# Two memory-attention layers and two linear-attention layers on one core: other queues, places and release points for stores and loads

## The chip, the core and the metric

The kernel runs on one core of a Trainium2 chip. The core has a matrix engine (TensorE, PE in the profile, with its weight loads shown as PEld), a vector engine (VectorE, DVE), a scalar engine (ScalarE, ACT), a general engine (GpSimd, POOL) and a synchronisation engine (SyncE, SP), which here only issues DMAs. DMAs are also issued by ScalarE and GpSimd. The metric is the device time of one execution in microseconds (us); lower is better.

## The reference

The input `x` has 2048 rows of 640 values. Four layers follow one another, A B A B, each on a layer norm of its input and with its input added to its output.

```python
# layer A: recurrent memory attention, 32 heads of 192, 64 segments of 32 rows, 8 memory rows
mem = mem0
for s in range(n_seg):
    h = concatenate([mem, x[segment s]])              # 8 + 32 rows
    q, k, v = h @ Wq, h @ Wk, h @ Wv                  # per head
    p = softmax(where(mask, q k^T * scale, -1e9))
    o = (p v, all heads) @ Wo
    mem = o[:8]                                       # goes into the next segment
    outs.append(o[8:])
# layer B: linear attention with softmax features, over all rows at once
```

So the segments of an A layer form a chain: segment s+1 needs the first eight output rows of segment s. Layer B has no such chain.

## The kernel before

An A layer has two stages. `A_pre` is the batched stage. In it the kernel computes, for eight rows of every segment (the border rows, whose input does not depend on the memory), the keys, queries and values of all segments in large matmuls, and puts them into DRAM: keys and queries into `kqb_d`, values into `vb_d`. `A_chain` is the chain. It goes through the 64 segments one after another, each in four rounds of eight heads; every other segment takes the rounds in reverse order.

The batched stage. `keys_and_queries(h, r)` makes the keys and queries of half h of the segments for round r: 120 matmuls (L985), evictions by VectorE and ScalarE in turn (L94 and L96, through `evict`), and one store of 1.5 MB to `kqb_d` (L993). Eight of them run in each A layer, mixed with four `first_values`, which make the border values of the first segments. In the first layer the stage also does the layer norm of all 2048 rows in 16 blocks: `norm_tasks` cuts a block into four steps (load of the rows at L926, moments, deviation, applying at L302 and store to `xn` at L927), and `evict` does one such step after each eviction. The normed block stands in a tile `ln_xn`. GpSimd issues the block's load and store. In the third layer the rows were normed before.

Also in the first layer, `lay_out_wo` (L812 to L816) rewrites the output weights `Wo` in DRAM, 32 DMAs from SP, into the order in which the chain reads them (`wo_rows`); `early_wo` and `late_wo` load parts of that (L774) into SBUF (the large tile is called `arena`). `fetch_first_rows` (L1000) is SP's DMA that brings the first segment's normed rows into `under`. At the start of the chain VectorE transposes them into `hT` (L1081), copies the kept tokens into `tT` (L1082), and prepares the banks of the first queries and keys (L1090).

A segment of the chain. Per round, `project` (L1137 to L1159) multiplies `hT` with the weights of queries, keys and values: five steps (b = 0 to 4, one for each 128 rows of the weights) of four matmuls each (L1154). Then come ScalarE's copies of the raw rows (L1169, L1181), transposes (L1174), scores (L1191), the weighted values (L1204), the turning of the result (`turn`, with L1382 for round 1, which writes it into the buffer `vt`), and the product with `Wo` (L1263), which collects in `ps_w`. The segment ends with the sum of that product (L1457), which gives the next `hT` (L1459). GpSimd fetches the border keys and queries of a round (`load_kqb`, L1123), copies them beside the others (L1130), and fetches the border values into `Vp` (L1134).

Streamed weights. Of four rounds' weights most stay in SBUF. Three of Q's five row blocks, two of K's and two of V's of the first and last round share seven slots (`SLOTS`, `load_slot`, L748), and four pieces of `Wo` share a region as well (`load_piece`, L797). So each segment loads 11 pieces again, for its last round. They are put in the list `held`, in the order Q, Q, Q, K, K, V, V and four of `Wo`, and `release` takes the next from the list: SP's DMA then waits for a given matmul. `PACE` says at which step: `("Q", 1): 4` means that after step 4 of the projection of Q in round 1 one load is released.

Border values of later segments. They are computed during the chain by `next_values` (into the bank `ps_x`). `keep_values` (L1301) copies them by ScalarE (L1304) into `vt` and gives back a function that stores `vt` into `vb_d` (L261, SP's queue). At the start of a segment the copy stands first, ahead of the summed rows (`keep_rows`, L1112), the tails (`tail_rows`, L1247) and the first query rows; the store is issued behind the projection of Q. This happens in 112 segments of the two chains.

The order of instructions on each engine is that in which the program issues them; an engine waits at an instruction until what it needs is there, and everything behind it on that engine waits too.

Of the kernel before, what the change touches and what calls it, by code (L numbers as in the profile page):

```python
# [8 lines left out]
P = 128  # L9
BF16 = mybir.dt.bfloat16  # L10
# [12 lines left out]

VH = 194

PACE = {("Q", 0): 0, ("K", 0): 1, ("V", 0): 3, ("Q", 1): 4, ("K", 1): 4, ("V", 1): 3, ("Q", 2): 1, ("K", 2): 0, ("V", 2): 0,
        ("Q", 3): 0, ("K", 3): 0}

STEPS = (2, 5)

# [92 lines left out]
class Kernel:  # L123
# [712 lines left out]
    def A_pre(self, xn_dram, li, load_matrix, piece, wo_mid, wo_end, lay_out_wo, early_wo, x_raw):  # L836


        nc, tc, ev, KC, NSEG = self.nc, self.tc, self.ev, self.KC, self.NSEG
        NR = 4  # L840
        SH = min(NSEG, 32)
# [8 lines left out]
        with ExitStack() as es:  # L850
            ps_ = es.enter_context(tc.tile_pool(name=f"A{li}_preps", reuse_waits="tile", bufs=8, space=bass.MemoryType.PSUM))
            if x_raw is not None:
                lp = es.enter_context(tc.tile_pool(name=f"A{li}_preln", reuse_waits="tile", bufs=2))
# [27 lines left out]
            def norm_tasks(load, done, tag="ln_xn"):  # L881

                v = {}

                def a():
                    v["x"] = lp.tile([P, self.Dm], BF16, name="ln_x", bufs=3)
                    load(v["x"])

                def b():
                    v["m"] = self.ln_moments(lp, v["x"])  # L890

                def c():
                    v["d"] = self.ln_deviation(lp, v["m"])

                def d():
                    xn = lp.tile([P, self.Dm], BF16, name=tag, tag=tag)
                    self.ln_apply(lp, v["x"], v["m"], v["d"], xn[:])
                    done(xn)

                return [a, b, c, d]  # L900
# [72 lines left out]
            def keys_and_queries(h, r):  # L973
                nonlocal turn
                st = sts[turn % 2]
                turn += 1
                xBT = columns(h)
                for mi, m in enumerate("KQ"):
                    w = [piece(m, r, b) for b in range(KC)]
                    for c0 in range(0, 12, CB):  # L980
                        ps = ps_.tile([P, 512], F32, name="ps_pre", tag="bank")
                        for i in range(CB):
                            c = c0 + i
                            for b in range(KC):
                                nc.tensor.matmul(ps[:, T * i:T * i + T], lhsT=w[b][:, P * c:P * c + P], rhs=xBT[:, b, :],  # L985
                                                 start=(b == 0), stop=(b == KC - 1))
                        G, xi = c0 // 6, c0 % 6
                        so = st[:, :, 96 * mi:96 * mi + 96]
                        so = (so.rearrange("p s (i g t) -> p i g s t", g=2, t=8) if m == "K" else
                              so.rearrange("p s (i t g) -> p i g s t", g=2, t=8))  # L990
                        evict(out=so[:, xi:xi + CB, G],
                              in_=ps[:, :].rearrange("p (i t s) -> p i s t", i=CB, t=8))
                nc.scalar.dma_start(out=self.kqb_d[r, :, SH * h:SH * h + SH, :], in_=st)  # L993

            def load_round(r):
                for m in "KQV":
                    load_matrix(m, r)

            def fetch_first_rows():
                nc.sync.dma_start(out=self.first_rows(), in_=self.rows_of(0))  # L1000

            if x_raw is not None:
                load_round(3)
                load_round(2)
                rows_ready(0)
                tasks += tails(1)
                keys_and_queries(0, 3)
                rows_ready(1)
                tasks += all_rows()
                keys_and_queries(1, 3)  # L1010
                first_values(3)
                self.build_A_consts()
                load_round(1)
                load_round(0)
                for r in (0, 2, 1):
                    lay_out_wo([r])
                early_wo(True)
                lay_out_wo([3])
                fetch_first_rows()
                keys_and_queries(0, 2)  # L1020
                keys_and_queries(1, 2)
                first_values(2)
                keys_and_queries(0, 1)
                keys_and_queries(1, 1)
                first_values(1)
                keys_and_queries(0, 0)
                first_values(0)
                keys_and_queries(1, 0)
                early_wo(False)
            else:  # L1030
                load_round(0)
                rows_ready(0)
                load_round(2)
                keys_and_queries(0, 0)
                first_values(0)
                self.build_A_consts()
                keys_and_queries(0, 2)
                rows_ready(1)
                keys_and_queries(1, 0)
                load_round(3)  # L1040
                load_round(1)
                early_wo(True)
                fetch_first_rows()
                keys_and_queries(1, 2)
                first_values(2)
                keys_and_queries(0, 3)
                keys_and_queries(1, 3)
                first_values(3)
                load_round(0)
                keys_and_queries(0, 1)  # L1050
                first_values(1)
                keys_and_queries(1, 1)
                early_wo(False)
# [4 lines left out]
    def A_chain(self, xn_dram, at_dram, li, load_slot, piece, late_wo, load_both, wo, low):  # L1058
        nc, tc, KC, NSEG = self.nc, self.tc, self.KC, self.NSEG
        scale = float(self.Dh) ** -0.5  # L1060
        NR = 4
        with tc.tile_pool(name=f"A{li}_ch", reuse_waits="tile", bufs=1) as sp, \
# [74 lines left out]
            def project(hT, ps, m, n, s, steps):  # L1137
                order = rounds(s)
                r = order[n]
                ns = SLOTS[m]  # L1140
                for i in steps:
                    b = (i + KC - ns) % KC if n == 0 else i
                    w = piece(m, r, b)
                    for g in range(4):
                        if m == "V":
                            hp = 2 * (g % 2) + g // 2
                            rhs = w[:, 384 * hp:384 * hp + 384]
                        else:
                            w3 = w[:, 32 * g:32 * g + 32]
                            rhs = ap3(w3, [list(w3.ap[0]), [P, 6], [768, 2], [1, 32]])  # L1150
                        o = ps[32 * g:32 * g + 32, 0:384]
                        if m != "V":
                            o = ps[32 * g:32 * g + 32, :].rearrange("p (x c) -> p x c", x=2)[:, :, 64 * (g // 2):64 * (g // 2) + 192]
                        last = nc.tensor.matmul(o, lhsT=hT[:, b, :], rhs=rhs, start=(i == 0),  # L1154
                                         stop=(i == KC - 1), tile_position=(0, 32 * g), skip_group_check=True)
                    if n == 0 and b >= KC - ns:
                        self.held.append(lambda b=b: load_slot(m, order[NR - 1], b))
                    if PACE.get((m, n)) == i:
                        self.release(last)  # L1159
# [12 lines left out]
            def turn_rows(pairs):  # L1172
                for o, i in pairs:
                    nc.vector.transpose(out=o, in_=i)  # L1174
# [126 lines left out]
            def keep_values():  # L1301
                if waiting:
                    ps, k, unit = waiting.pop()
                    nc.scalar.activation(out=self.two_heads(vt), in_=ps[:, 0:384].rearrange("p (e f) -> p e f", e=2), func=ACT.Copy)  # L1304
                    return lambda: self.store_values(nc.sync, vt, k, *unit)
# [24 lines left out]
            for s in range(NSEG):  # L1330
# [4 lines left out]
                def q_or_k(m, n, halves=False):  # L1335
                    ps = psk if m == "K" else psq
                    project(hT, ps, m, n, s, range(KC))
                    return to_rows(ps, m, halves)
# [7 lines left out]
                    elif s + 1 < NSEG:  # L1346
                        extra_v(s + 1, n + 2 - NR)

                store = None
                if s > 0:  # L1350
                    store = keep_values()
                    keep_rows(W_done)
                    rows = tail_rows(rct, spare_rows())
                    otb = turn_tail(rows)
                    store_rows(s - 1)
                    store_tail(otb, s - 1, rounds(s - 1)[L])
                raw = q_or_k("Q", 0)
                if store:
                    store()
                turn_rows(raw)  # L1360
                turn_rows(q_or_k("K", 0))
                if s == 0:
                    late_wo(3, range(OWN // 2))
                pv = v_banks()
                project(hT, pv, "V", 0, s, range(KC))
                v_rows(pv, 0, "sv")
                turn_tails(s)
                OTs = []
# [186 lines left out]
```

## Time and profile before

| | us |
|---|---|
| median of 3 runs | 3292.88 (3291.52 to 3293.26) |
| the profiled execution | 3279.86 |
| span in its trace | 3278.1 |
| TensorE busy | 3043.7 |
| VectorE busy | 2157.5 |
| ScalarE busy | 1901.7 |
| GpSimd busy | 1384.0 |

The span is the time from the first to the last instruction in the trace; the execution's own time is 1.76 us more. The mean granted clock of TensorE is 0.986 of full speed. A line such as L1154 is a line of the kernel printed above. Rows of waits give an engine and line, what it waited for, the total in us, how often, and the longest. Rows of a timeline give the start in us, the duration, the engine, the line, the operation, the tiles (out<-in), the count, and in brackets the idle time before it and what ended it. A row of a window gives its bounds, its length, the busy time of TensorE, its weight loads, VectorE, ScalarE and GpSimd, each with a count, TensorE's clock, the busy share of the DMA engines and GB/s.

### The profile page before, as it was taken

The numbers are of one execution on the slowest core, as the hardware profiler recorded it, in microseconds if no ns is written. First come the engines' busy times: TensorE is split into PE (matmuls) and PEld (weight loads), VectorE is DVE, ScalarE is ACT, GpSimd is POOL, SyncE is SP. The second block draws the span as 40 slices with busy tenths as digits, with TensorE's granted clock in tenths as the row PEclk, the third lists the DMA queues.
The fourth block names the chain that finished last, engine by engine and source line by source line (L and its number), as shares of the span: only waits on it lengthen the run. The fifth ranks groups of instructions, "written<-read, shape, count | busy, mean of one in ns | idle before, by whom it ended". The sixth has DMA issues, their size and how long they took to land.

```text
span 3278.1 us, 141616 instructions
## 1 busy us (share of the span) xinstructions
PE 3043.7 (93%) x59586; PEld 1930.3 (59%) x59586; DVE 2157.5 (66%) x5425; ACT 1901.7 (58%) x4537; POOL 1384.0 (42%) x2856
## 2 busy tenths in 40 slices
PE   8799999999999999999999999999999999998999
PEld 6555566566566555555467566665566565655553
DVE  5466677677677667746654666667677667776565
ACT  2256666666666666646443566666666666665463
POOL 2254455445554454530121554545454545454300
PEclk9899999999999999999999999999999999999999
DMA  9877777777777777760268777777777777777400
GB/s 376 294 267 237 234 254 253 235 243 259 243 243 257 243 236 247 258 224 3 97 222 325 259 243 238 242 253 245 231 245 257 245 239 245 259 237 265 158 1 33
DMA packets 338750, 749.67 MB, mean 229 GB/s; under 512 B 68538, under 2 KB 115250, under 8 KB 335042
## 3 DMA queue, kind: packets, MB, share of 16 engines
q1 hardware_dynamic: 268258, 637.09, 56.2%
q0 software_dynamic: 66976, 77.87, 8.6%
q10 hardware_dynamic: 2880, 25.66, 1.9%
q8 instruction: 469, 7.68, 0.9%
q14 instruction: 167, 1.37, 0.1%
HBM read 670.77 MB, written 78.01 MB: 228 GB/s over the span
## 4 chain that ended last, share of the span: by engine, by line
PE 60%; DMA 25%; DVE 7%; issue 3%; ACT 3%; POOL 0%; SPq 0%; POOLq 0%; DVEq 0%; ACTq 0%
DMA arena<-in_A_Wv_dram 17%; PE ps_qk_q L1154 9%; PE ps_w L1263 9%; PE ps_v L1154 9%; PE ps_qk_k L1154 8%; PE ps_pre L985 5%; PE ps_s L1191 4%; PE kv L1510 2%; DMA vb<-under 2%; PE ps_o L1204 2%; DVE raws L1457 2%; PE ps_wo L466 2%; DMA Vp<-vb 2%; DMA arena<-in_A_Wk_dram 1%; PE ps_pq L517 1%
## 5 line engine op out<-in xcount | busy, mean ns | idle before, releaser
L1154 PEld LDWEIGHTS <-hT 128*32 128x32 bf16 x30720 | 801.6, 97 | 540.8 <-issue 98.0
L1174 DVE STREAM_TRANSPOSE QK<-raws 128x512 bf16<-128x512 bf16 (+1 forms) x1152 | 712.5, 634 | 133.1 <-ACT raws L1169 102.2
L1154 PE MATMUL ps_qk_q<-arena,hT 128*32 128x384 bf16 x10240 | 512.0, 328 | 54.1 <-DVE hT L1459 25.5
L1130 POOL COPY QK<-kqb 64x192 bf16<-64x192 bf16 x1024 | 351.9, 344 | 456.7 <-DMA kqb<-kqb 205.6
L1154 PE MATMUL ps_qk_k<-arena,hT 128*32 128x384 bf16 x10240 | 515.7, 328 | 6.4 <-DMA arena<-in_A_Wk_dram 3.8
L1154 PE MATMUL ps_v<-arena,hT 128*32 128x384 bf16 x8192 | 447.0, 328 | 43.0 <-DMA arena<-in_A_Wv_dram 35.1
L1169 ACT ACTIVATE raws<-ps_qk_k 128x512 bf16<-128x512 f32 (+1 forms) x640 | 313.6, 511 | 246.3 <-PE ps_qk_k L1154 240.1
L1234 ACT ACTIVATE raws<-ps_o,under 128x192 bf16<-128x192 f32 x1024 | 374.4, 421 | 119.4 <-DVE under L1228 98.9
L1134 POOL DMA_DIRECT2D Vp<-vb x512 | 258.9, 506 | 384.1 <-PE ps_t L1217 174.7
L1169 ACT ACTIVATE raws<-ps_qk_q 128x512 bf16<-128x512 f32 x512 | 305.0, 596 | 127.6 <-PE ps_qk_q L1154 116.1
L1183 DVE CAST Vp<-ps_v 64x384 bf16<-64x384 f32 x512 | 286.3, 559 | 71.4 <-ACT Vp L1181 57.8
L1263 PE MATMUL ps_w<-arena,under 128*32 128x320 bf16 x6144 | 310.0, 301 | 14.4 <-issue 11.8
L1123 POOL DMA_DIRECT2D kqb<-kqb x512 | 288.6, 564 | 68.4 <-POOL QK L1130 59.4
L1181 ACT ACTIVATE Vp<-ps_v 64x384 bf16<-64x384 f32 x512 | 247.1, 483 | 91.3 <-PE ps_v L1154 89.3
L1191 PEld LDWEIGHTS <-QK 128*80 128x80 bf16 x4096 | 196.8, 121 | 162.8 <-issue 152.4
L1191 PE MATMUL ps_s<-QK 128*80 128x80 bf16 x4096 | 255.0, 210 | 6.5 <-POOL QK L1130 2.9
L1273 ACT ACTIVATE E<-ps_s 80x320 bf16<-80x320 f32 x512 | 218.0, 426 | 37.3 <-PE ps_t L1217 36.9
L1119 POOL DMA_DIRECT2D attn<-under x128 | 91.5, 715 | 339.6 <-DVE under L1115 317.5
L985 PEld LDWEIGHTS <-arena 128*128 128x128 bf16 x1920 | 189.3, 99 | 43.1 <-issue 15.3
L1304 ACT ACTIVATE under<-ps_x 128x384 bf16<-128x384 f32 x112 | 55.1, 492 | 273.3 <-PE ps_x L257 273.3
L1204 PE MATMUL ps_o<-Vp,E 80*32 80x193 bf16 x4096 | 181.6, 249 | 23.3 <-DMA Vp<-vb 10.9
L1263 PEld LDWEIGHTS <-under 128*32 128x32 bf16 x6144 | 149.5, 96 | 45.2 <-issue 19.9
(167 smaller groups left out, 4378.8 us busy)
## 6 DMA issues: line engine op xcount, KB each, us to landing
arena<-wo_rows SPq DMA_DIRECT2D x560, 320.0 KB, 6.2
arena<-in_A_Wq_dram SPq DMA_DIRECT2D x427, 384.0 KB, 6.2
arena<-in_A_Wk_dram SPq DMA_DIRECT2D x298, 384.0 KB, 6.5
arena<-in_A_Wv_dram SPq DMA_DIRECT2D x290, 384.0 KB, 7.0
kqb<-arena ACTq DMA_DIRECT2D x16, 1536.0 KB, 9.4
kqb<-kqb POOLq DMA_DIRECT2D x512, 48.0 KB, 5.0
Vp<-vb POOLq DMA_DIRECT2D x512, 24.2 KB, 4.7
otb<-otb POOLq DMA_DIRECT2D x256, 48.0 KB, 4.4
```

Source lines behind the costliest of these rows:

```text
L985: nc.tensor.matmul(ps[:, T * i:T * i + T], lhsT=w[b][:, P * c:P * c + P], rhs=xBT[:, b, :], start=(b == 0), stop=(b == KC - 1))
L1123: nc.gpsimd.dma_start(out=kqb[:], in_=self.kqb_d[r, :, s, :])
L1130: nc.gpsimd.tensor_copy(out=o, in_=kqb[h, :].rearrange("p (x c q) -> p x c q", c=3, q=16))
L1134: nc.gpsimd.dma_start(out=Vs[n % 2][64:80, :], in_=self.vb_d[s // 8, r].rearrange("g (t s) x f -> s (g t) (x f)", s=8)[s % 8])
L1154: last = nc.tensor.matmul(o, lhsT=hT[:, b, :], rhs=rhs, start=(i == 0), stop=(i == KC - 1), tile_position=(0, 32 * g), skip_group_check=True)
L1169: nc.scalar.activation(out=raw[:, c], in_=ps[:, c], func=ACT.Copy)
L1174: nc.vector.transpose(out=o, in_=i)
L1183: nc.vector.tensor_copy(out=o, in_=i)
L1191: nc.tensor.matmul(S[0:80, c0:c0 + 80], lhsT=KT[:, 4 * x + c, :], rhs=QT[:, 4 * x + c, :], start=(c % 2 == 0), stop=(c % 2 == 1), skip_gro ...
L1204: nc.tensor.matmul(O[G][32 * h:32 * h + 32, VH * G:VH * G + 193], lhsT=E[0:80, 80 * h + 32 * G:80 * h + 32 * G + 32], rhs=V[0:80, VH * h:V ...
L1234: nc.scalar.activation(out=out, in_=i, func=ACT.Copy, scale=rc[G])
L1263: step = nc.tensor.matmul(W[q:q + 32, 0:320], lhsT=OT[i // 6][:, i % 6 // 2, 32 * (i % 2):32 * (i % 2) + 32], rhs=rhs, start=(first and i ...
```

## The change

It does five things.

1. `PACE`: the releases at Q of round 1, and K and V of round 1 come at steps 3, 1 and 1 in place of 4, 4 and 3; those at K and V of round 2 and Q and K of round 3 at step 3 in place of 0.
2. The tile `ln_xn` of the first layer's layer norm has three buffers in place of two.
3. The 16 stores of keys and queries to `kqb_d` (L993) are issued by GpSimd in place of ScalarE.
4. `fetch_first_rows` is called earlier: in the first layer ahead of the 32 DMAs of `lay_out_wo`, in the third ahead of `early_wo(True)`. The order of the laying out stays (rounds 0, 2, 1, then 3).
5. `keep_values` is called after the keys of the first round in place of the segment's start, so that ScalarE copies the border values behind the first keys' rows; the store follows the projection of V on SP, behind the third load of Q.

```diff
-PACE = {("Q", 0): 0, ("K", 0): 1, ("V", 0): 3, ("Q", 1): 4, ("K", 1): 4, ("V", 1): 3, ("Q", 2): 1, ("K", 2): 0, ("V", 2): 0,
-        ("Q", 3): 0, ("K", 3): 0}
+PACE = {("Q", 0): 0, ("K", 0): 1, ("V", 0): 3, ("Q", 1): 3, ("K", 1): 1, ("V", 1): 1, ("Q", 2): 1, ("K", 2): 3, ("V", 2): 3,
+        ("Q", 3): 3, ("K", 3): 3}
...
-                    xn = lp.tile([P, self.Dm], BF16, name=tag, tag=tag)
+                    xn = lp.tile([P, self.Dm], BF16, name=tag, tag=tag, bufs=3 if tag == "ln_xn" else 2)
...
-                nc.scalar.dma_start(out=self.kqb_d[r, :, SH * h:SH * h + SH, :], in_=st)
+                nc.gpsimd.dma_start(out=self.kqb_d[r, :, SH * h:SH * h + SH, :], in_=st)
...
                 load_round(0)
-                for r in (0, 2, 1):
-                    lay_out_wo([r])
+                fetch_first_rows()
+                lay_out_wo((0, 2, 1))
                 early_wo(True)
                 lay_out_wo([3])
-                fetch_first_rows()
...
                 load_round(1)
+                fetch_first_rows()
                 early_wo(True)
-                fetch_first_rows()
...
-                store = None
                 if s > 0:
-                    store = keep_values()
                     keep_rows(W_done)
...
-                raw = q_or_k("Q", 0)
-                if store:
-                    store()
-                turn_rows(raw)
+                turn_rows(q_or_k("Q", 0))
                 turn_rows(q_or_k("K", 0))
+                store = keep_values()
                 if s == 0:
                     late_wo(3, range(OWN // 2))
                 pv = v_banks()
                 project(hT, pv, "V", 0, s, range(KC))
+                if store:
+                    store()
```

## The prediction

> **What bounds the kernel now.** I read the page's busy times first, then its chain, then the waits of TensorE, because the share of an engine says little where stages differ.
>
> ```profile
> span 3278.1 us, 141616 instructions
> PE 3043.7 (93%) x59586; PEld 1930.3 (59%) x59586; DVE 2157.5 (66%) x5425; ACT 1901.7 (58%) x4537; POOL 1384.0 (42%) x2856
> DMA arena<-in_A_Wv_dram 17%; PE ps_qk_q L1154 9%; PE ps_w L1263 9%; PE ps_v L1154 9%; PE ps_qk_k L1154 8%; PE ps_pre L985 5%; PE ps_s L1191 4%; PE kv L1510 2%; DMA vb<-under 2%; PE ps_o L1204 2%; DVE raws L1457 2%; PE ps_wo L466 2%; DMA Vp<-vb 2%; DMA arena<-in_A_Wk_dram 1%; PE ps_pq L517 1%
> ```
>
> TensorE is busy 93%, so at most 3278.1 - 3043.7 = 234.4 us of its idle time can go. The chain gives the value weights' DMA 17%, but a chain counts a transfer's whole flight; what it costs is TensorE's wait at its end:
>
> ```profile
> PE ps_v L1154 <- DMA arena<-in_A_Wv_dram: 35.1, 65, 1.7
> ...
> PE ps_qk_q L1154 <- DVE ps_qk_q L1090: 18.8, 2, 18.3
> ...
> PE ps_pre L985 <- ACT arena L96: 6.6, 4, 2.1
> PE ps_pre L985 <- DVE arena L94: 6.2, 2, 4.5
> ...
> PE ps_qk_k L1154 <- DMA arena<-in_A_Wk_dram: 3.8, 10, 0.8
> ```
>
> (Columns: total us, times, longest.) Two of these rows can be reached by the change: one wait of 18.3 us, and 75 small ones for streamed weights, 35.1 + 3.8 = 38.9 us. The large one is the border between the first layer's batched stage and its chain:
>
> ```profile
> 128.67 13.28 PE L985 MATMUL ps_pre<-arena 128*128 128x256 bf16 x120
> ...
> 160.21 1.79 PE L1154 MATMUL ps_qk_q<-arena,hT 128*32 128x384 bf16 x20 [18.26 <-DVE ps_qk_q L1090]
> ...
> 188.85 1.58 PE L1154 MATMUL ps_qk_q<-arena,hT 128*32 128x384 bf16 x20
> ```
>
> TensorE finishes its last batch at 141.95 and stands 18.26 us. The row names VectorE's L1090, but that is only last in a series; VectorE itself waits for the first rows, which SP issues last:
>
> ```profile
> 158.00 0.35 DVE L1081 STREAM_TRANSPOSE hT<-under 128x160 bf16<-128x160 bf16 x1 [16.37 <-DMA under<-xn]
> ...
> 81.65 44.73 SPq L816 DMA_DIRECT2D wo_rows<-in_A_Wo_dram  x24
> ...
> 138.28 15.13 SPq L816 DMA_DIRECT2D wo_rows<-in_A_Wo_dram  x8
> 153.53 0.66 SPq L1000 DMA_DIRECT2D under<-xn  x1
> 154.39 5.19 SPq L774 DMA_DIRECT2D arena<-wo_rows  x8
> ```
>
> Behind the issue at 153.53 lie its flight, L1081 and L1090 to 160.21. And SP is late partly because it waits for ScalarE's stores of keys:
>
> ```profile
> SPq L816 <- DMA kqb<-arena: 29.8, 3, 11.1
> ...
> SPq L774 <- DMA kqb<-arena: 13.2, 2, 9.9
> ...
> L993 ACTq DMA_DIRECT2D kqb<-arena x16: 326/327/358, 26.7 to 1785.4; - x16
> ```
>
> No L816 transfer shares data with those stores. In the built program SP's and ScalarE's DMAs take their completion marks in turn from one set of eight, and an issue waits until the DMA eight places back has landed; GpSimd's draw on a set of their own. So a store that ScalarE issues only at a batch's end holds up SP's next eight.
>
> **The change, part by part.** *First rows sooner, first layer.* L1000 goes ahead of all 32 lay-outs, to about 81.65 instead of 153.53. What it needs is long there: the first block of normalised rows is stored at 35.3 (the L927 row below). L1081 then runs among the last batches, and the chain starts when the last batch ends. The price of that border is shown by the third layer, where the rows were already early:
>
> ```profile
> 1785.17 1.00 PE L1154 MATMUL ps_qk_q<-arena,hT 128*32 128x384 bf16 x20 [0.58 <-DVE ps_qk_q L1090]
> ...
> 1814.71 1.03 PE L1154 MATMUL ps_qk_q<-arena,hT 128*32 128x384 bf16 x20
> ```
>
> Term: 18.26 - 0.58 = **-17.7**. Cover gone, what is late next? The loads that used the pause. The first segment lasts 188.85 - 160.21 = 28.6 in the first layer and 1814.71 - 1785.17 = 29.5 in the third, where nothing was paused before it; so without the pause I expect the same 29 us, which DMA volume sets: **0** (-3 to +1). For that SP must be on time. The eight L774 loads at 154.39 now follow lay-outs without the 29.8 + 13.2 us of waits (the L816 ones and most of L774's lie in this stage), so they can be issued near 125, if their targets are free. Were they not sooner, they would be the next wait: the refill rival below.
>
> *Key stores on GpSimd's queue; a third `ln_xn` buffer.* The 16 issues leave ScalarE: 16 x 0.33 = 5 us of an engine that is 58% busy, nothing by itself. What counts are its waits in the first stage:
>
> ```profile
> POOL xn L927 <- DVE ln_xn L302: 52.4, 12, 8.9
> ...
> ACT ln_lv L289 <- DMA arena<-in_A_Wk_dram: 9.3, 1, 9.3
> ...
> DVE ln_xn L302 <- DMA xn<-ln_xn: 12.1, 4, 7.5
> ...
> ACT arena L96 <- DMA arena<-in_A_Wk_dram: 7.0, 2, 5.4
> ...
> POOL Vp L1134 <- DMA vb<-arena: 6.0, 1, 6.0
> L927 POOL DMA_DIRECT2D xn<-ln_xn x16: 542/547/606, 35.3 to 115.6; - x16
> ```
>
> Layer-norm steps run between evictions (L94, L96), so VectorE's 7.5 us wait for a buffer and ScalarE's 9.3 and 5.4 for weight loads (the same eight marks) hold evictions, and TensorE's waits for them in L985 are 6.6 + 6.2 = 12.8 us, in both layers. The upper end of the gain is these 12.8; the other end is a loss: on GpSimd's queue `xn` stores and `ln_x` loads now stand behind a 1.5 MB store of 9.4 us flight (section 6 row below), which could give two of the L302 waits back, +6. I take **-5**, nearer the gain, because both waits have a named remover. Issue on GpSimd is costed at 0.55 each, as L927's, 9 us in all on an engine that is 42% busy.
>
> Weighed against this is the Trainium skill, "SBUF — State Buffer", section "A bandwidth-pool intuition that's wrong": a GpSimd-issued DMA beside a two-port VectorE copy went from about 620 to about 3100 ns. By it, as an estimate, 16 stores cost 16 x 2.5 = 40 us of GpSimd, of which the one ahead of the chain would matter. L927's longest, 606 ns beside a busy VectorE, disagrees with it, so I leave it out of the sum.
>
> *The same in the third layer.* Rows never waited for there (the 0.58 above); ScalarE's store leaves SP, but the last store stands on GpSimd behind the chain's first row fetches, some eight issues and copies of about L927's 0.55 = 4 us later. It is read only by later key fetches of its own round. **-1** (-2 to +4, the whole delay).
>
> *The chains: 128 segments, in 112 of which a border store is made.* From the timelines of one segment, which begins at 228.14, its start on TensorE, SP's first issues, the rewriting of `vt` and the last V row; then two of its windows, and the flight of V's loads in two stretches; last the page's row of the border copy:
>
> ```profile
> 228.14 1.00 PE L1154 MATMUL ps_qk_q<-arena,hT 128*32 128x384 bf16 x20 [0.15 <-DVE hT L1459]
> ...
> 228.53 0.33 SPq L748 DMA_DIRECT2D arena<-in_A_Wq_dram  x1
> 228.97 0.50 SPq L261 DMA_DIRECT2D vb<-under  x1
> 229.57 1.40 SPq L748 DMA_DIRECT2D arena<-in_A_Wq_dram  x2
> ...
> 238.07 0.59 DVE L1382 STREAM_TRANSPOSE under<-raws 128x192 bf16<-128x192 bf16 x2
> 241.34 0.35 PE L1154 MATMUL ps_v<-arena,hT 128*32 128x384 bf16 x4 [0.16 <-DMA arena<-in_A_Wv_dram]
> ...
> 232.60:234.10 1.50, 1.50 (x52) 1.07 (x44) 0.98 (x3) 1.07 (x3) 0.59 (x2) 1.00 0.63 138
> 234.10:241.50 7.40, 7.24 (x180) 4.55 (x172) 6.01 (x16) 5.51 (x15) 3.45 (x9) 1.00 1.03 379
> ...
> arena<-in_A_Wv_dram SPq DMA_DIRECT2D x2, 384.0 KB, 6.9
> arena<-in_A_Wv_dram SPq DMA_DIRECT2D x12, 384.0 KB, 5.7
> ...
> L1304 ACT ACTIVATE under<-ps_x 128x384 bf16<-128x384 f32 x112 | 55.1, 492 | 273.3 <-PE ps_x L257 273.3
> ```
>
> Of the windows, the last two columns are DMA's share and GB/s. The queue is full from 234.10 (1.03) until the last streamed V row lands, at 241.34. The new pace releases K's two rows and V's first one to three steps sooner (a step is a fifth of a 1.00 us projection), but V's last, the one waited for, keeps its point (`Q2`, step 1). Sooner loads can only fill the gap of 37% x 1.50 = 0.55 us at 232.60; the wo pieces come 0.6 later. In the other direction works the border store: it moves from behind the first to behind the third Q load, still ahead of that V row, so the same bytes precede it. Of the last two rows, the first is from such a segment, the second from the end of the chain, where no border store is made: 6.9 against 5.7 us. That 1.2 us is its price, paid before and after. Bounds: -38.9 if all waits for streamed V and K vanish; on the other side, below under R3, +39. I take **-3**, near zero, as the point that decides is unchanged. ScalarE's border copy (L1304) moves behind K's rows; TensorE has V and the next Q to multiply over it: nothing, and at most its 55.1 us if V's rows became the bound, for which no row of the waits speaks.
>
> Sum: -17.7 + 0 - 5 - 1 - 3 = **-26.7**. The profiled execution took 3279.9, 13.0 under the median of the runs, 3292.9; it goes to 3253.2, and the median to **3266**.
>
> **The rivals.** *R1, the chains gain too.* If the filled gap of 0.55 us carries through to the last V row, TensorE's 65 waits, mean 35.1 / 65 = 0.54, vanish: 3266 - 39 + 3 = 3230. For it: the gap is as long as the mean wait. Against: a full queue behind it, and a store moved into it.
>
> *R2, the pause is refilled.* The stores free nothing: late wo rows, or the first `Vp` and `kqb` fetches (6.0 above), take the place of the 18.26. Then only the -5 or so stays: **3288**. For it: SP still lays out 32 pieces, and eight loads come after them; against: the third layer's 0.58.
>
> "DMA: Bandwidth & Descriptors" of the Trainium skill, section "Issuing engines are not separate DMA queues", speaks for R2: issuing from several engines saves only the issue time, 16 x 0.33 us here. SP's 29.8 us of waits for ScalarE's stores are a cost that this rule does not count.
>
> *R3, slower: the border store is late.* `vt`, which it reads, is written anew by L1382 at 238.07, 9.93 into the segment. Behind three Q loads its issue is near 231.1; with the flight of its neighbours, 6.2 to 6.9 (Wq's in section 6; Wv above), it is done at 237.3 to 238.0, so 0.1 to 0.8 us of slack is left. If it lands later, VectorE stops at L1382, with all turns and evictions queued behind it; or the V row comes later by as much. This decides from 26.7 / 112 = 0.24 us a segment; at 0.35 it costs +39 and gives 3266 + 39 = **3305**. Against: a store need only be read from its source in time, and 97 KB is a quarter of a load.
>
> ```profile
> arena<-in_A_Wq_dram SPq DMA_DIRECT2D x427, 384.0 KB, 6.2
> kqb<-arena ACTq DMA_DIRECT2D x16, 1536.0 KB, 9.4
> ```
>
> **How the numbers follow.** The forecast 0.54 (own range 3252 to 3281: the unknown terms, -12.8 to +6 and about 10 of the chain, added as independent), R1 0.15, R2 0.15, R3 0.16. 0.2%, about what a measurement here can tell from no change, is 6.6 us: 3286.3 to 3299.5 counts as the same. Faster: 0.52 of the forecast, 0.15 of R1, 0.05 of R2, **0.72**; same: 0.02, 0.10 of R2 and 0.01 of R3, **0.13**; slower **0.15**. The range that leaves out half of R1 and most of R3: **3235 to 3292**.
>
> **What would show it.** Right: L1081 without a wait near 90 to 130, TensorE's wait before the first Q of the chain under 2 us, the first segment 27 to 30 us, no SP row that waits for `kqb<-arena`, L302's 7.5 and the 4.5 of L985 gone. Chains: V waits still 25 to 40 us; R1 if under 10. R2: a wait of over 5 us for `Vp`, `kqb` or `wo_rows` within the first segment. R3: VectorE's L1382 waiting for `vb<-under`, or V waits above 60 us. Wrong altogether, if L1000's issue itself stands on SP for an `xn` store and holds the lay-outs behind it.

## The result, and the profile after

The changed kernel takes 3255.66 us (median of 4 runs, 3246.43 to 3256.29) against 3292.2 us (3283.38 to 3293.26, 4 runs): 36.5 us less, a ratio of 0.9888 with a 95% interval of 0.9864 to 0.9913. The prediction, 3266 in 3235 to 3292, holds it. In another set of runs, on one of the chips of the experiments, the gain was smaller (0.9969, below): the kernel before was there some 22 us faster and the changed one was not. The two profiled executions, 3279.86 and 3255.99, differ by 23.9 us; the steps are compared in these.

From the page of after, its span and busy times; then the largest waits of TensorE (total us, times, longest):

```profile
span 3254.1 us, 141518 instructions
PE 3041.1 (93%) x59552; PEld 1929.3 (59%) x59586; DVE 2180.9 (67%) x5425; ACT 1897.0 (58%) x4537; POOL 1387.7 (43%) x2872
```

```profile
PE ps_o L1203 <- DMA Vp<-vb: 27.8, 32, 2.0
PE ps_v L1153 <- DMA arena<-in_A_Wv_dram: 23.6, 54, 1.6
PE ps_s L1190 <- POOL QK L1129: 20.1, 30, 3.1
PE ps_qk_q L1153 <- DVE hT L1456: 20.0, 46, 1.1
PE ps_pre L985 <- DVE arena L94: 14.9, 2, 8.6
```

(Lines of the chain have moved up by one to three.) The 18.8 us before the first Q are gone from the top. Two rows are new there: waits for border values, `Vp`, and for GpSimd's copy of border keys. Before, they were far smaller:

```profile
PE ps_o L1204 <- DMA Vp<-vb: 10.9, 14, 1.9
...
PE ps_s L1191 <- POOL QK L1130: 2.9, 8, 1.4
```

V's weights cost 23.6 us in place of 35.1.

The border of the first layer on TensorE's timeline: last batch, first queries of the chain, the first scores, the last wait of the first segment, first queries of the second segment:

```profile
132.39 13.27 PE L985 MATMUL ps_pre<-arena 128*128 128x256 bf16 x120
146.24 1.00 PE L1153 MATMUL ps_qk_q<-arena,hT 128*32 128x384 bf16 x20 [0.58 <-DVE ps_qk_q L1089]
...
152.94 0.23 PE L1190 MATMUL ps_s<-QK 128*80 128x80 bf16 x1 [3.05 <-POOL QK L1129]
...
175.62 0.99 PE L1262 MATMUL ps_w<-arena,raws 128*32 128x320 bf16 x12 [0.73 <-DMA arena<-wo_rows]
...
179.51 1.00 PE L1153 MATMUL ps_qk_q<-arena,hT 128*32 128x384 bf16 x20
```

The pause fell from 18.26 to 0.58, as forecast. But the batch ends at 132.39 + 13.27 = 145.66, 3.7 later than before, and the first segment lasts 179.51 - 146.24 = 33.3 in place of 28.6. Of the 17.7 us only 188.85 - 179.51 = 9.3 are left at its end. New in this segment are the waits for border keys and values at its start, some 4 us; the waits for rows of `Wo` at its end, 5.3 us in all, were 4.8 before.

Where the 23.9 us arose, from the starts of segments on TensorE's timelines (the first Q row after each new `hT`):

| | before | after | gain |
|---|---|---|---|
| start to the second segment of the first chain | 188.85 | 179.51 | 9.3 |
| from there to its last segment's start | 1189.9 | 1189.2 | 0.8 |
| to the second chain's start (layer B, third layer's batches) | 406.4 | 406.7 | -0.3 |
| second chain, first to last segment's start | 1222.2 | 1208.3 | 13.9 |
| rest | 270.7 | 270.5 | 0.2 |

The chains hide two large changes of opposite sign. I sorted the segments 2 to 55 of both chains by their number: the 96 whose number is not a multiple of 8 last 19.16 us on the mean before and 18.75 after; the 12 whose number is a multiple of 8 last 19.76 before and 22.13 after. Over segments 1 to 62 of both chains, the 110 plain ones gain 0.44 each, 49 us, and the 14 eighth ones lose 2.3 each, 33 us.

What is special in an eighth segment: there the border values of the next eight segments are used for the first time. The last of their eight parts (half a round each) is copied and stored at the start of that very segment, and GpSimd's fetch of round 2 (L1133) reads it some microseconds later. GpSimd in the eighth segment that starts at 311.22 in after:

```profile
315.12 0.74 POOL L1129 COPY QK<-kqb 64x192 bf16<-64x192 bf16 x2 [0.87 <-PE ps_s L1190]
321.74 0.52 POOL L1133 DMA_DIRECT2D Vp<-vb  x1 [5.88 <-PE ps_qk_q L1153]
322.25 0.56 POOL L1122 DMA_DIRECT2D kqb<-kqb  x1
322.86 0.74 POOL L1129 COPY QK<-kqb 64x192 bf16<-64x192 bf16 x2
```

SP in the same segment, with the border store behind all three Q loads:

```profile
311.61 2.44 SPq L748 DMA_DIRECT2D arena<-in_A_Wq_dram  x3
314.16 0.50 SPq L261 DMA_DIRECT2D vb<-under  x1
```

And TensorE, which waits first for the copy of keys queued behind that fetch, then for the fetch itself:

```profile
323.25 0.23 PE L1190 MATMUL ps_s<-QK 128*80 128x80 bf16 x1 [1.58 <-POOL QK L1129]
...
326.36 0.51 PE L1203 MATMUL ps_o<-Vp,E 80*32 80x193 bf16 x8 [1.32 <-DMA Vp<-vb]
```

The fetch is issued 10.5 us into the segment, after GpSimd stood idle for 5.88 us. The row names a TensorE instruction as what ended the wait, because only some of the completion marks of SP's DMAs are recorded and the view then knows no landing for the border store. The trace's records of marks, which no view prints, tell more: in all 14 eighth segments, before and after, an instruction in front of this fetch waits for that one of SP's marks which the segment's border store sets. Before, the store is issued 0.8 to 0.9 us into the segment and the fetch 7.3 to 8.1; after, 2.9 to 3.4 and 9.4 to 11.3.

TensorE's clock takes part in the loss. Behind these waits the granted clock stands at half (0.50, third number from the end), and a projection takes 1.84 us in place of 0.99:

```profile
326.30:329.20 2.90, 2.84 (x40) 1.67 (x41) 1.42 (x4) 0.88 (x3) 1.68 (x4) 0.50 0.31 111
```

```profile
327.17 1.84 PE L1153 MATMUL ps_v<-arena,hT 128*32 128x384 bf16 x20
```

Such stretches, 3.4 or 6.8 us long, lie in 8 of the 14 eighth segments of after, 34.1 us together, and in 1 of the 110 plain ones; in before they lie in 2 of the 14, 6.8 us together, and in 6 of the 110. If work at half clock takes twice as long, (34.1 - 6.8) / 2 = 13.7 us, as an estimate and at most, of the 33 us lost are clock, and the rest the waits themselves.

### The profile page after: what moved, and what is told of

The parts are those of the page before. It is cut to its first block, busy times and chain, and to the rows that moved or that the text cites. A ratio compares the mean times of both kernels' runs of the same rounds, so it can differ in the third digit from the quotient of the medians.

```text
span 3254.1 us, 141518 instructions
## 1 busy us (share of the span) xinstructions
PE 3041.1 (93%) x59552; PEld 1929.3 (59%) x59586; DVE 2180.9 (67%) x5425; ACT 1897.0 (58%) x4537; POOL 1387.7 (43%) x2872
## 5 line engine op out<-in xcount | busy, mean ns | idle before, releaser
L1173 DVE STREAM_TRANSPOSE QK<-raws 128x512 bf16<-128x512 bf16 (+1 forms) x1152 | 729.5, 642 | 219.6 <-ACT raws L1168 163.6
L1153 PE MATMUL ps_v<-arena,hT 128*32 128x384 bf16 x8192 | 448.5, 330 | 28.9 <-DMA arena<-in_A_Wv_dram 23.6
L1133 POOL DMA_DIRECT2D Vp<-vb x512 | 257.9, 504 | 372.8 <-PE ps_t L1216 204.1
L1111 ACT ACTIVATE raws<-ps_w 64x160 f32<-64x160 f32 x256 | 76.9, 300 | 245.3 <-DVE raws L1454 243.8
L985 PEld LDWEIGHTS <-arena 128*128 128x128 bf16 x1920 | 190.6, 100 | 47.8 <-issue 18.8
L1223 DVE RECIPROCAL under<-ps_o 128x2 f32<-128x2 f32 x384 | 65.7, 171 | 176.9 <-PE ps_o L1203 173.0
```

The costliest lines, as they stand in the source:

```text
L1133: nc.gpsimd.dma_start(out=Vs[n % 2][64:80, :], in_=self.vb_d[s // 8, r].rearrange("g (t s) x f -> s (g t) (x f)", s=8)[s % 8])
```

## The experiments

Three chips were used; the kernel before took 3273.52 us on the first (19 runs), 3269.65 on the second (19 runs) and 3299.15 on the third (7 runs). Each time is compared with the runs of before on its own chip.

**One part alone.** Part 4, first rows sooner:

```diff
-                for r in (0, 2, 1):
-                    lay_out_wo([r])
+                fetch_first_rows()
+                lay_out_wo((0, 2, 1))
                 early_wo(True)
                 lay_out_wo([3])
-                fetch_first_rows()
...
+                fetch_first_rows()
                 early_wo(True)
-                fetch_first_rows()
```

> The kernel before with part 4 alone (first rows fetched sooner in both A layers). The sum's theory: TensorE's wait at the first layer's border falls from 18.26 to about 0.6 us, and with the key stores still on ScalarE some 3 to 6 us of it come back as waits in the first segment: 12 to 15 us faster than before, about 3278. The refill rival (SP still waits 43 us for ScalarE's stores, so the wo rows come late): 0 to 4 us faster, with TensorE's waits for wo_rows in the first segment above 10 us.

Measured: 3270.44 us (10 runs), ratio 0.9984 (0.9965 to 1.0003). The border in its trace:

```profile
137.83 1.00 PE L1153 MATMUL ps_qk_q<-arena,hT 128*32 128x384 bf16 x20 [0.58 <-DVE ps_qk_q L1089]
...
150.13 1.10 PE L1190 MATMUL ps_s<-QK 128*80 128x80 bf16 x8 [8.59 <-POOL QK L1129]
...
161.50 0.46 PE L1262 MATMUL ps_w<-arena,under 128*32 128x320 bf16 x4 [4.00 <-DMA arena<-wo_rows]
...
182.15 1.00 PE L1153 MATMUL ps_qk_q<-arena,hT 128*32 128x384 bf16 x20
```

The pause is gone and the chain starts 22.4 us sooner (4.7 of them because the batched stage ended sooner), but the first segment lasts 44.3 us: the refill rival, though its waits for rows of `Wo` come to 7.8 us and not to the 10 expected. 8.59 us more are the wait for border keys, whose copy stands on GpSimd behind a fetch of border values that waits 4.46 us for its store; before, this ran within the pause.

Part 5, the border copy and store later (the change's last hunk):

> The kernel before with part 5 alone (border copy behind the first keys, its store behind the third Q load). Theory, from the trace of after, where every eighth segment lasts about 22 us and the others 18.7: the store is read by GpSimd's fetch of Vp in the same segment when the segment's number is a multiple of 8, so those 14 segments become 2 to 3 us longer (+28 to +42 us), and the other 98 gain at most 0.2 us each from ScalarE's 0.49 us (-20 to 0): 3300 to 3330, slower. Rival: the copy's move is what makes the other segments 0.4 us shorter (-40), so that the sum is about nothing: 3285 to 3295.

Measured: 3312.85 us, ratio 1.0118 (1.0073 to 1.0162): slower, by 39 us, as the first theory had it. Eighth segments last 22.60 us on the mean, plain ones 19.00. The chains of its trace, the fastest of its four runs, are 25 us longer than those of before; where the other 14 us of the medians lie is not shown. Its waits show the same two rows as after does:

```profile
PE ps_v L1154 <- DMA arena<-in_A_Wv_dram: 44.1, 76, 1.9
PE ps_o L1204 <- DMA Vp<-vb: 30.0, 28, 2.4
...
PE ps_s L1191 <- POOL QK L1130: 19.4, 28, 2.1
```

Part 1, the new `PACE` alone:

> The kernel before with part 1 alone (PACE). Theory: the sooner releases of K's rows and V's first make the plain segments of the chain shorter, by 0.2 to 0.4 us in 124 segments: 25 to 45 us faster, 3247 to 3267, with TensorE's waits for V's weights under 15 us. The prediction's own theory: the last V row's release is unchanged, so the chain stays within 5 us: 3287 to 3297, V's waits 30 to 40 us.

Measured: 3265.45 us, ratio 0.9973 (0.9957 to 0.9989), 8 us faster; plain segments 19.11, V's waits 39.4 us. Neither expectation: nearly nothing, as the prediction had it for the chain, V's waits too. Yet part 5 alone gives 0.16 us a plain segment and part 1 alone 0.04, and both together 0.41.

**The eighth segments.** The kernel after, with the old order in these alone:

```diff
                 if s > 0:
+                    if s % 8 == 0:
+                        store = keep_values()
                     keep_rows(W_done)
...
-                turn_rows(q_or_k("Q", 0))
+                raw = q_or_k("Q", 0)
+                if store:
+                    store()
+                turn_rows(raw)
```

> The kernel after, but in segments whose number is a multiple of 8 the border copy and its store stay at their places of before (copy first on ScalarE, store behind the first Q load). Theory of the late reader: 14 segments fall from about 22 to 19 to 20 us, 28 to 40 us faster than after: 3215 to 3228. Rival (these segments are long because new border tokens are loaded and turned there): within 5 us of after, 3250 to 3260.

Measured: 3225.58 us, ratio 0.9856 (0.9817 to 0.9894), 48 us faster than before on that chip. Eighth segments last 19.52 us, plain ones 18.80. GpSimd in the eighth segment from 309.92:

```profile
313.87 0.75 POOL L1129 COPY QK<-kqb 64x192 bf16<-64x192 bf16 x2 [0.41 <-PE ps_s L1190]
317.61 0.52 POOL L1133 DMA_DIRECT2D Vp<-vb  x1 [3.00 <-PE ps_s L1190]
```

Here the store was issued 2.1 us sooner, 0.84 into the segment in place of 2.94:

```profile
310.31 0.34 SPq L748 DMA_DIRECT2D arena<-in_A_Wq_dram  x1
310.76 0.50 SPq L261 DMA_DIRECT2D vb<-under  x1
```

The fetch follows at 7.7 us in place of 10.5, 2.8 sooner, and of the 14 eighth segments only one still holds a stretch at half clock. New border tokens are loaded in these segments as before, so that rival falls: the late reader of the store is shown. (After itself did not run on this chip; the two are set side by side below.)

On the second chip three more kernels ran beside after itself.

> The changed kernel itself, so that the other three have it on the same chip: 25 to 40 us faster than before, as measured (ratio 0.9888).

Measured: 3259.16 us (10 runs), ratio 0.9969 (0.9955 to 0.9983): 10.5 us, less than expected. The trace repeats: chain start 145.70, second segment at 180.38, eighth segments 21.87, plain 18.70.

**The key stores.** After with part 3 undone:

```diff
-                nc.gpsimd.dma_start(out=self.kqb_d[r, :, SH * h:SH * h + SH, :], in_=st)
+                nc.scalar.dma_start(out=self.kqb_d[r, :, SH * h:SH * h + SH, :], in_=st)
```

> The kernel after with the 16 key stores back on ScalarE (part 3 undone). Theory: the stores on GpSimd hold up the loads of the layer norm behind them, so without them the first layer's batched stage ends 5 to 9 us sooner than in after (chain start near 138 to 141 in place of 146.2), but SP waits 25 to 40 us for ScalarE's stores again and the first segment grows from 33 to 40 to 45 us: within 8 us of after, either way. The prediction's theory (stores on GpSimd make the stage shorter by 5 us and keep the first segment short): 10 to 20 us slower than after.

Measured: 3265.37 us (10 runs), ratio 0.9985 (0.9965 to 1.0004), whose interval overlaps that of after. SP's waits for the stores are back at 32.2 us, and so is a short batched stage. In after 15.4 us of them had stayed, all in L774 (last row):

```profile
SPq L816 <- DMA kqb<-arena: 17.3, 2, 9.7
SPq L774 <- DMA kqb<-arena: 9.8, 2, 6.5
SPq L755 <- DMA kqb<-arena: 5.1, 1, 5.1
```

```profile
SPq L774 <- DMA kqb<-arena: 15.4, 3, 9.7
```

```profile
135.14 1.00 PE L1153 MATMUL ps_qk_q<-arena,hT 128*32 128x384 bf16 x20 [0.58 <-DVE ps_qk_q L1089]
...
179.08 1.20 PE L1153 MATMUL ps_qk_q<-arena,hT 128*32 128x384 bf16 x20
```

The chain starts 11 us sooner than in after and its second segment at the same time, 179.08 against 179.51; the first segment lasts 43.9 us. Moving the stores shifted waits; at the end of the first segment it was worth nothing.

**Two repairs of the border,** both on top of the early copy in eighth segments. First, border keys ahead of border values on GpSimd:

```diff
+            extra_kq(kqs.pop(0))
             extra_v(0, 0)
             extra_v(0, 1)
-            extra_kq(kqs.pop(0))
```

> The kernel with the early copy in every eighth segment, and at the start of the chain GpSimd copies the first border keys before it fetches the first border values (which wait for a store of values). Theory: TensorE's wait of 3.05 us for L1129's copy in the first segment goes, and part comes back as a wait for Vp: 0 to 3 us from each chain's first segment, the first one at 29 to 32 us; in all 0 to 6 us faster than that kernel, 30 to 40 us faster than after. Rival: the wait for Vp takes it all, first segment again 32.7.

Measured: 3222.56 us, ratio 0.9861 (0.9835 to 0.9887), 37 us faster than after on that chip. The first segment did not shorten (34.6 us, second segment at 180.40): TensorE still waited 3.96 us for the copy, and 2.12 for `Vp`. The rival held; the time is that of the early copy. GpSimd's rows show why:

```profile
144.62 0.81 POOL L261 DMA_DIRECT2D vb<-arena  x1 [4.58 <-ACT arena L96]
145.42 1.16 POOL L1122 DMA_DIRECT2D kqb<-kqb  x2
153.13 0.74 POOL L1129 COPY QK<-kqb 64x192 bf16<-64x192 bf16 x2 [6.55 <-DMA kqb<-kqb]
```

The copy waits for its own keys. Their fetch stands behind a store of border values, which stood until an eviction was done.

Then also the layer norm's loads on ScalarE:

```diff
-                return in_turn([norm_tasks(lambda x, q=q: nc.gpsimd.dma_start(out=x[:], in_=x_raw[q, :]),
+                return in_turn([norm_tasks(lambda x, q=q: nc.scalar.dma_start(out=x[:], in_=x_raw[q, :]),
```

> As the run before, and the first layer's layer-norm loads (L926) are issued by ScalarE in place of GpSimd. Theory: what lengthens the batched stage in after is that these loads stand behind stores on GpSimd's queue that wait (VectorE waits 38.5 us for them); then VectorE's wait for ln_x falls under 12 us and the chain starts 4 to 9 us sooner, near 138 to 142. Rival: the waits sit with the stores of normed rows and the evictions themselves, so the start stays at 145 to 147.

Measured: 3229.58 us, ratio 0.9873 (0.9846 to 0.9899). VectorE's waits for `ln_x`, up to the chain's first segment, in after and then in this kernel:

```profile
DVE ln_stats L278 <- DMA ln_x<-in_A_x_dram: 38.5, 9, 13.9
```

```profile
DVE ln_stats L278 <- DMA ln_x<-in_A_x_dram: 11.9, 4, 5.8
```

The chain started at 137.32, against 145.85 in the run before, as the theory said: the loads behind waiting stores on GpSimd's queue are what made the stage longer. But the second segment began at 180.29 once more (TensorE's wait for the copy of keys grew from 3.96 to 11.55 us), and the time is no lower than that of the run before.

**What sets the end of the first segment?** On the third chip, after without the laying out of round 3:

```diff
-                nc.sync.dma_start(out=into, in_=self.wo_rows[r, :, 1280 * k:1280 * k + 1280])
+                nc.sync.dma_start(out=into, in_=self.wo_rows[min(r, 2), :, 1280 * k:1280 * k + 1280])
...
                 lay_out_wo((0, 2, 1))
                 early_wo(True)
-                lay_out_wo([3])
```

> The kernel after without the last 8 of the 32 laying-out transfers (round 3's output weights, 2 MB; round 3 reads round 2's rows in their place, so the output is another one and the loads are as many). Theory: the volume that DMA must move until the first segment needs its last wo rows sets that segment's end (DMA share 0.78 to 1.04 throughout; first segment's end at 179.5 in after, and 179 to 182 in three other kernels whose chain starts between 135 and 146): 2 MB at some 366 GB/s are 5.4 us, so the end falls to 173 to 176. Rival: the end is set by waits for border keys and values and the order at the border: 178.5 to 180.5.

Measured (one run, 3251.89 us): the second segment begins at 178.17, 1.3 sooner than in after. The share of DMA from 120 to 140 fell from 0.85 to 0.67 (the last two columns of the windows are DMA's share and GB/s; after first, then this kernel):

```profile
120.00:140.00 20.00, 20.00 (x189) 17.22 (x187) 7.59 (x13) 6.12 (x10) 4.28 (x6) 1.00 0.85 316
...
160.00:170.00 10.00, 7.69 (x192) 4.96 (x181) 5.90 (x17) 5.30 (x15) 4.31 (x10) 1.00 0.99 364
```

```profile
120.00:140.00 20.00, 20.00 (x188) 17.22 (x187) 8.18 (x15) 5.84 (x10) 4.92 (x7) 1.00 0.67 237
...
160.00:170.00 10.00, 6.92 (x128) 4.17 (x121) 4.74 (x15) 4.43 (x13) 3.62 (x9) 0.83 1.03 388
```

So the volume moved earlier is not the limit; my theory of 5.4 us falls. From 160 to 170 DMA is full (0.99, 1.03) in both, with loads that are released only within the segment. In all nine traces whose chain starts between 135 and 147, TensorE's last waits in the first segment are for such loads of `wo_rows`, 3.1 to 8.0 us together. That they set the end is a reading that these rows allow; it was not tried.

After with part 2 undone:

```diff
-xn = lp.tile([P, self.Dm], BF16, name=tag, tag=tag, bufs=3 if tag == "ln_xn" else 2)
+xn = lp.tile([P, self.Dm], BF16, name=tag, tag=tag)
```

> The kernel after with two ln_xn buffers again (part 2 undone). Theory: since the first segment's end is set by something later, the third buffer is worth nothing at that end (179 to 181, as in after), and the median is within 4 us of after (3255 to 3263 on this chip). The prediction's theory: VectorE's wait for xn stores comes back, 5 us slower.

Measured: 3248.97 us, ratio 0.9856 (0.9827 to 0.9886) on the third chip, where after itself did not run; so the median can't be set against it. VectorE's waits for stores of normed rows are back, as the prediction's theory said (none in after):

```profile
DVE ln_xn L302 <- DMA xn<-ln_xn: 16.1, 3, 8.7
```

But its waits for `ln_x` fell to 23.8 us, the chain starts at 145.03 (146.24 in after) and the second segment at 180.53: the third buffer is worth nothing there.

Last, the chains of the kernel with the early copy, with the border of before (parts 1 and 5 with the early copy; parts 2 to 4 left out):

> The kernel before with parts 1 and 5 alone, and with the early copy in every eighth segment: the chains of the fast kernel with the border of before. Theory: plain segments at 18.7 to 18.85 us and eighth ones at 19.2 to 19.8 as there; first segment's end near 188 as in before; the time is 8 to 12 us over that of the kernel with all parts and the early copy (3222 to 3226), so 3232 to 3238, 32 to 40 us under before. Rival: the chains' gain needs the key stores off ScalarE too (marks shared with SP): plain segments 19.0 or more, 3255 or more.

Measured: 3219.97 us, ratio 0.976 (0.9722 to 0.9797) on the third chip. That is 79 us under before on that chip, where 32 to 40 were expected. Plain segments 18.76, eighth 19.48, second segment at 186.69. Its time is as low as those with all parts. As the chips differ in the kernel before by up to 29.5 us, this does not price parts 2 to 4; it shows that the chain's shorter plain segments need none of them.

## Why the prediction was right, point by point

The time lay 10 us under the forecast, inside the range, and of the 26.7 us forecast for the profiled execution 23.9 came. That the sum lies so near is luck. Up to the second segment of the first chain it counted on 22.7 us and 9.3 came; from the chains it counted on 3, and 15.9 came.

- *First rows sooner, -17.7.* Right for the wait, 18.26 to 0.58. L1080's transposition ran at 119.53 without a wait. As a gain it was too large: 9.3 us stayed at the end of the first segment.
- *First segment, "0 (-3 to +1)".* Wrong, +4.6. The step that failed was to take the third layer's first segment as the price without a pause. There the border values of round 0, with which the chain begins, are computed first of the four rounds; in the first layer they come last, and their store stands right in front of GpSimd's first fetches. The pause had hidden that wait; it came out as 8.59 us in the run with part 4 alone and 3.05 + 0.87 us in after. This is half of the refill rival, with border keys as the wait. In nine traces whose chain starts between 135 and 147, the second segment began between 178.2 and 182.2.
- *Key stores and third buffer, -5.* Wrong in sign, +3.7. The loss that the text named as the other bound, loads behind a 1.5 MB store on GpSimd, was the one that occurred (38.5 us of VectorE's waits after 6.8), and the run with these loads on ScalarE took it away. SP's waits did fall, but not to nothing as the text had it: L774 still waited 15.4 us for these stores. That can't be the shared marks any more, since the stores now set GpSimd's; their source and the target of those loads both lie in `arena`. So the eight loads forecast near 125 were issued from 130.86 to 146.0.
- *Third layer, -1.* Wrong in sign, but small: +1.3 in its first segment, +0.3 ahead of it (layer B included).
- *Chains, -3.* The traces give -15.9 without the third layer's first segment, out of some 49 gained and 33 lost. "As the point that decides is unchanged" failed: with the store behind the Q loads and K's and V's releases sooner, TensorE multiplies the last streamed V row at 13.47 us into a plain segment (mean) in place of 13.64, and waits for it 0.24 in place of 0.34; the rest of the 0.41, some 0.25, comes behind it. So a part of R1 happened. Parts 5 and 1, each alone, leave 13.71 and 13.75. Why they need each other was not settled.
- *R3, "the border store is late".* Its mechanism happened and was named with the wrong reader. VectorE's L1379 waited once, for 0.8 us; the slack of 0.1 to 0.8 us I had given it was enough. The one who waits is GpSimd's fetch in every eighth segment, which reads what was just stored; I had counted writers of `vt` and not readers of `vb_d`. Alone part 5 made the kernel 39 us slower. That this is R3's price is chance: R3 had counted 112 segments at 0.35 us, and here 14 segments lose some 2.8 each while the others gain.

The two rules of the Trainium skill can be held against the runs. "DMA: Bandwidth & Descriptors", section "Issuing engines are not separate DMA queues", would have the move of the stores change almost nothing; in time that agrees (0.9985 and 0.9969 with overlapping intervals), though the trace shows waits of some 10 us moving between queues, which the rule does not tell. "SBUF — State Buffer", section "A bandwidth-pool intuition that's wrong", would have made GpSimd's issues about 3 us beside a two-port copy of VectorE; in after the 16 took 531 to 612 ns (whether such a copy ran beside them is not shown):

```profile
L993 POOL DMA_DIRECT2D kqb<-arena x16: 531/566/612, 25.6 to 1779.6; - x16
```

## What to carry to other kernels

When a store is moved back, list who reads its target as well as who rewrites its source, and look at the iteration where the newest piece is read first: a cost in one of eight iterations does not show in a median. A pause that an early load removes may have covered other work; look at what waited within it, and judge at the next common point rather than at the pause. Keep the good order in the plain iterations and the old one in the special ones: three kernels with the early copy in every eighth segment beat the kernel before on three chips (0.9856, 0.9861 and 0.976 of its time), and one of them beat the changed one by 37 us where both ran side by side.

## What was not expected of the hardware

The kernel before took 3273.5, 3269.7, 3292.2 and 3299.2 us (medians) in four sets of runs on several chips, while the changed one took 3255.7 and 3259.2 in two of them: the gain of the same change was 36.5 us in one and 10.5 in the other, each outside the other's interval. Whether the chip or something else of a set makes the difference is not shown.
